# Gated linear attention and a two-layer network on one core: loads without the padding rows, four stores in halves, another fixed order of steps

## The chip, the cores and the metric

The kernel runs on one core of a Trainium2 chip. The metric is device time in microseconds for one execution, on the chip, lower being better. Five engines work beside each other, each in its own fixed order: TensorE (PE, with its weight loads as PEld), VectorE (DVE), ScalarE (ACT), GpSimd (POOL) and SyncE (SP). SP issues the loads and stores here. Semaphores order the engines against each other.

## The reference

Four sequences of 768 tokens with 8 heads of 48 channels go through a recurrence; then all 3072 tokens, 384 wide, go through two dense layers.

```python
for t in range(S):                                  # S = 768; state is [B, H, 48, 48]
    state = alpha[:, :, t, :, None] * state + einsum('bhd,bhe->bhde', k[:, :, t], v[:, :, t])
    y[:, :, t] = einsum('bhd,bhde->bhe', q[:, :, t], state)
x = y.transpose(0, 2, 1, 3).reshape(3072, 384)
h = x @ w_in                                        # 384 -> 2048, weights in float64
g = h * erf(softplus(h))
out = (g @ w_out).astype(float32)                   # 2048 -> 384
```

## The kernel before

The recurrence is computed in chunks of 64 tokens. There are 24 chunk steps (`n` 0 to 23): two pairs of sequences by twelve chunks, and one step holds 128 token rows. A chunk step loads alpha, k, q and v (`la`, `lk`, `lq`, `lv`); two scans over alpha (`sb`, `sa`) give the decay after and up to each token, and k and q are multiplied by them in place (`kk`, `qq`). On TensorE `ps` makes the scores, `qt` and `sv` the outputs from the state and from the chunk's own tokens, `pn` turns k, and `pu` makes the state's update. On VectorE `mk` masks the scores (tile `sT`), `td` decays the state. `kn` and `kd` copy k out, `ta` adds the update. `xh` copies the output's rounded part to `x_hi`; its rest comes either by `xp` on TensorE and `xe` on ScalarE, or by `xl` on VectorE.

Two chunk steps make a block of 256 tokens for the dense layers; there are twelve blocks. Each value is held as a rounded part (`hi`) and a rest (`lo`), so each layer is three products. The 2048 inner columns stand in four groups, each in two halves. `hm_b_g_half` makes half a group of `h` for block b in 18 matmuls of 256 columns, into one of two PSUM tiles. `he` (ScalarE) or `hd` (VectorE) copies it out. `u`, `n1`, `n2`, `n3` and `g` are ScalarE's passes for the nonlinear function, `ma`, `mb`, `z1` and `z2` VectorE's (tiles `s`, `w`, `t`, `hs`). `ga` or `gd` rounds half a group, `gl` takes the rest, and `om_b_g_half` adds 12 matmuls of 384 columns to the block's two accumulators. `oe` or `ob` copies an accumulator out and `od` stores 128 rows of it. `u` and `g` need one function table in ScalarE, `n1` to `n3` another; `need` loads a table wherever the program asks for the other one.

The weights come as float64, in 12 tiles of 128 x 4096 bytes and 16 of 128 x 3072. Each is loaded (`wl`), its high bits copied (`wd`, ScalarE, tile `top`), joined with the low bits (`wa`, VectorE), rounded (`wh` on ScalarE, `wk` on VectorE), and its rest taken: by `wq` on VectorE, or by `wp` on TensorE with `we` on ScalarE. A letter behind these names says which matrix, i or o. `dw` are matmuls of the identity alone, in the gaps of the start.

The order is written out by hand, or by a planner outside of the program: the table ORDER lists all 1605 steps, and the loop at the end calls them one by one. Each engine's instructions stand in the order of these calls, and a chain of dependencies (`Queue.call`, line 204) forbids any other, so SP, too, issues its loads in table order; a load whose tile is still read makes all later ones wait. Nearly every instruction is recorded through that one line, so in the profile rows are told apart by tiles: `h__115` and `h__116` are the PSUM tiles of `hm`, `pn` and `wp`, `acc` those of `om`, `both` that of `ps` and `pu`, `py` that of `qt`, `sv` and `xp`.

Channels are padded from 48 to 64. For alpha, k and q a chunk is 128 rows of channels, with padding in rows 48 to 63 and 112 to 127. For v a row is a token and 8 heads of 64 columns, 16 of them padding.

Of the kernel before, what the change touches and what calls it, by code (L numbers as in the profile page):

```python
# [31 lines left out]
sv_0 wdi_3 pn_0 whi_1 wai_3 wpi_2 la_1 wli_4 xh_0 sb_1 rc_1 xp_0 dw_1 lk_1 kn_0 wdi_4 lq_1 xe_0 wli_0 sa_1 kk_1 wei_2
whi_3 pn_1 qq_1 wqi_1 wai_4 lv_1 pu_0 wlo_3 wdi_0 ps_1 kn_1 whi_4 dw_1 mk_1 ta_0 sv_1 wli_5 pu_1 wdo_3 wai_0 whi_0
wqi_3 wdi_5 xh_1 la_2 ta_1 wao_3 wqi_4 wpi_0 ic_1 wei_0 xp_1 wli_7 sb_2 xe_1 wlo_10 who_3 lq_2 wai_5 rc_2 td_2 wdi_7
sa_2 wai_7 whi_5 hm_0_0_0 qq_2 hm_0_0_1 wli_6 qt_2 lk_2 ic_2 wdo_10 wli_8 wli_9 wao_10 he_0_0_0 kk_2 la_3 lv_2 wdi_6
# [884 lines left out]
```

## Time and profile before

| | us |
|---|---|
| median of 3 runs (506.89 to 510.46) | 507.69 |
| the profiled execution | 507.52 |
| its span, first to last instruction | 505.7 |
| TensorE busy | 495.0 |
| VectorE busy | 478.3 |
| ScalarE busy | 463.0 |
| of it 78 table loads | 100.1 |
| POOL busy | 6.2 |

The span is shorter than the execution's time by what lies before the first instruction and behind the last. A matmul's end is modelled, and matmuls overlap; the distance between the starts of two rows tells more than a row's length. The 16 DMA engines are busy throughout from 5 to 30 us, while the weights come, and by 32% from 40 to 50 us; behind 100 us their share stays under 30%.

### The profile page before, as it was taken

What the parts mean: (1) busy time and instruction counts of PE and PEld (TensorE: products, weight loads), DVE (VectorE), ACT (ScalarE), POOL (GpSimd) and SP (SyncE); (2) the same over time, 40 slices, a digit from 0 to 9 for tenths busy, and PEclk for the clock granted to TensorE, in tenths of its full rate; (3) what the DMA queues carried; (4) which work ended last, traced back from release to release, by engine and by line L of the source; (5) the groups of instructions that cost most, each with busy time, mean ns of one, the idle gap of its engine ahead of it and who ended that gap; (6) DMA issues with size and microseconds to landing.
All of it is one profiled execution on the core that took longest, in us unless ns stands there. A gap on an engine that the chain in (4) does not pass through costs nothing.

```text
span 505.7 us, 16774 instructions
## 1 busy us (share of the span) xinstructions
PE 495.0 (98%) x7418; PEld 473.6 (94%) x7418; DVE 478.3 (95%) x643; ACT 463.0 (92%) x609; POOL 6.2 (1%) x39
## 2 busy tenths in 40 slices
PE   7989999999999999999999999999999999999996
PEld 3689999999999999999999999999999999999996
DVE  6999999999999999999999999999899999689993
ACT  4999999999999899989999999977998899999971
POOL 2000000000000000000000000000000000000000
PEclk9999999999999999999999999999999999999999
DMA  8993663332103123012032122200313100000000
GB/s 290 403 365 84 211 209 107 97 107 72 40 29 111 43 63 126 22 27 97 1 101 81 44 81 96 64 21 21 105 46 110 44 1 34 1 1 31 1 32 34
DMA packets 21386, 43.68 MB, mean 86 GB/s; under 512 B 2368, under 2 KB 5440, under 8 KB 21312
## 3 DMA queue, kind: packets, MB, share of 16 engines
q1 hardware_dynamic: 21312, 42.59, 26.0%
q8 instruction: 59, 0.97, 0.8%
q14 instruction: 15, 0.12, 0.1%
HBM read 37.86 MB, written 4.72 MB: 84 GB/s over the span
## 4 chain that ended last, share of the span: by engine, by line
PE 41%; DVE 9%; ACT 8%; issue 2%; DMA 0%; DVEq 0%
PE acc L204 21%; PE h__116 L204 9%; PE h__115 L204 8%; PE py L204 2%; ACT L204 2%; PE both L204 2%; DVE t L204 1%; ACT w__100 L204 1%; ACT s__85 L204 1%; DVE A L204 1%; DVE gl__108 L204 1%; ACT s__89 L204 1%; ACT s__86 L204 1%; ACT w__99 L204 1%; DVE gl__107 L204 1%
## 5 line engine op out<-in xcount | busy, mean ns | idle before, releaser
L204 ACT ACT_TABLE_LOAD x78 | 100.1, 1283 | 2.2 <-PEq L874 0.9
L204 PE MATMUL acc<-wo_hi,gl__108 128*128 128x384 f32 x192 | 43.4, 338 | 0.1
L204 PE MATMUL acc<-wo_hi,gh__106 128*128 128x384 f32 x192 | 43.0, 337 | 0.0
L204 PE MATMUL acc<-wo_lo,gh__106 128*128 128x384 f32 x192 | 42.9, 337 | 0.0
L204 PE MATMUL acc<-wo_hi,gh__105 128*128 128x384 f32 x192 | 42.2, 339 | 0.0
L204 PE MATMUL acc<-wo_lo,gh__105 128*128 128x384 f32 x192 | 41.5, 336 | 0.0
L204 PE MATMUL acc<-wo_hi,gl__107 128*128 128x384 f32 x192 | 41.3, 336 | 0.0
L204 PEld LDWEIGHTS acc<-wo_hi,gl__108 128*128 128x128 f32 x192 | 34.1, 188 | 0.6 <-DVE gl__108 L204 0.4
L204 PEld LDWEIGHTS acc<-wo_lo,gh__106 128*128 128x128 f32 x192 | 34.3, 188 | 0.0
L204 PEld LDWEIGHTS acc<-wo_lo,gh__105 128*128 128x128 f32 x192 | 34.1, 188 | 0.0
L204 PEld LDWEIGHTS acc<-wo_hi,gl__107 128*128 128x128 f32 x192 | 34.0, 188 | 0.0
L204 PEld LDWEIGHTS acc<-wo_hi,gh__106 128*128 128x128 f32 x192 | 32.9, 188 | 0.2 <-ACT gh__106 L204 0.2
L204 PEld LDWEIGHTS acc<-wo_hi,gh__105 128*128 128x128 f32 x192 | 32.3, 188 | 0.5 <-DVE o__110 L204 0.3
L204 DVE TENSOR_TENSOR_SCAN B<-raw_a,back 128x520 f32<-128x520 f32 x24 | 29.6, 1233 | 1.7 <-DMA raw_a<-in_alpha_dram 1.6
L204 DVE TENSOR_TENSOR_SCAN A<-raw_a,start 128x520 f32<-128x520 f32 x24 | 29.6, 1233 | 0.1
L204 PE MATMUL h__115<-x_hi__112,wi_hi 128*128 128x256 f32 x156 | 23.4, 285 | 0.0
L204 ACT ACTIVATE s__87<-s__87 128x1024 f32<-128x1024 f32 x22 | 23.2, 1054 | 0.1
L204 PE MATMUL h__116<-x_hi__111,wi_lo 128*128 128x256 f32 x150 | 22.0, 281 | 1.1 <-issue 1.1
L204 PE MATMUL h__115<-x_hi__112,wi_lo 128*128 128x256 f32 x156 | 22.7, 281 | 0.0
L204 PE MATMUL h__116<-x_hi__111,wi_hi 128*128 128x256 f32 x150 | 22.7, 287 | 0.0
L204 PE MATMUL h__115<-x_lo__114,wi_hi 128*128 128x256 f32 x156 | 22.6, 280 | 0.0
L204 PE MATMUL h__116<-x_lo__113,wi_hi 128*128 128x256 f32 x150 | 21.8, 281 | 0.0
(370 smaller groups left out, 1364.4 us busy)
## 6 DMA issues: line engine op xcount, KB each, us to landing
raw_a<-in_alpha_dram SPq DMA_DIRECT2D x24, 260.5 KB, 2.8
raw_k<-in_k_dram SPq DMA_DIRECT2D x24, 256.0 KB, 3.3
raw_q<-in_q_dram SPq DMA_DIRECT2D x24, 256.0 KB, 3.6
raw_v__117<-in_v_dram SPq DMA_DIRECT2D x12, 256.0 KB, 3.9
raw_v__118<-in_v_dram SPq DMA_DIRECT2D x12, 256.0 KB, 4.0
out_dram<-o__110 SPq DMA_DIRECT2D x12, 192.0 KB, 3.2
out_dram<-o__109 SPq DMA_DIRECT2D x12, 192.0 KB, 2.0
s__85<-in_moe_w_out_dram SPq DMA_DIRECT2D x5, 384.0 KB, 5.6
```

Of the source, the lines that this page charges most:

```text
L204: ins = made(*args, **kw)
```

## The change

Three things change. (1) From chunk step 1 on, alpha, k and q are loaded into the first 112 partitions alone, so rows 112 to 127 keep what the first load or a memset put there; the k and q tiles of step 1 get their padding from POOL. The other padding, rows 48 to 63, is still loaded. The rows of v lose every second head's padding: 448 columns instead of 512. (2) The four stores of blocks 1 and 2 are each cut into two of 64 rows. (3) The table ORDER lists other steps in another order: `hd` 25 instead of 20 and `he` 71 instead of 76, `ob` 8 instead of 9 and `oe` 16 instead of 15, `wk` 1 instead of 5 and `wh` 27 instead of 23, `wp` 3 instead of 2 and `wq` 25 instead of 26, `xp` with `xe` 3 instead of 4 and `xl` 21 instead of 20. By the new order ScalarE loads a table 70 times instead of 78.

```diff
-la_0 sb_0 rc_0 wli_2 dw_4 sa_0 lk_0 wli_1 lq_0 wli_3 wdi_2 wai_2 kk_0 lv_0 qq_0 wdi_1 ic_0 whi_2 ps_0 wai_1 dw_1 mk_0
...
+la_0 lv_0 lk_0 lq_0 sb_0 rc_0 wli_3 dw_4 wdi_3 sa_0 wlo_10 wdo_10 kk_0 qq_0 wli_2 ps_0 la_1 wli_1 wli_0 pn_0 lk_1 mk_0
...
-    vs = Ring(raw, raw_v=([P, H * HD], F32, 2))
+    VH = HD + D
+
+    def vcol(pair, par):
+        return (pair // 2 * 2 + par) * VH + pair % 2 * HD
+
+    vs = Ring(raw, raw_v=([P, NP * VH], F32, 2))
...
+    for t in (rk[1], rq[1]):
+        nc.gpsimd.memset(t[P - 32 :], 0.0)
...
+        def part(self, out, in_):
+            rows = HD + D if self.n else P
+            sp.dma_start(out=out[:rows], in_=in_[:rows])
+
         def la(self):
-            sp.dma_start(out=ra, in_=alpha[self.m, self.c])
+            self.part(ra, alpha[self.m, self.c])
...
         def od(self, c):
-            sp.dma_start(out=out[bass.ds(self.tok + c * P, P), :], in_=self.o[c])
+            n = P // 2 if isinstance(self.tok, int) and self.tok // TB in (1, 2) else P
+            for at0 in range(0, P, n):
+                sp.dma_start(out=out[bass.ds(self.tok + c * P + at0, n), :], in_=self.o[c][at0 : at0 + n])
...
-            wide = _np.zeros((M, C, NI, TC, NP, 2, 64), a.dtype)
-            wide[..., :D] = a
+            a = a.reshape(M, C, NI, TC, NP // 2, 2, 2, D)
+            wide = _np.zeros((M, C, NI, TC, NP // 2, 2, 64 + D), a.dtype)
+            wide[..., :D], wide[..., 64:] = a[..., 0, :, :], a[..., 1, :, :]
```

`lk` and `lq` call `part` in the same way, and `sv` and `pu` read v by `vcol`.

SP's queue from its first load to the load of chunk step 1's q (`hs` and `s` are staging tiles of weights, 512 and 384 KB; `raw_k_122` and `raw_k_123` serve chunk steps in turn). Before:

```order
L204 DMA raw_a<-in_alpha_dram 128x521
L204 DMA hs__90<-in_moe_w_in_dram 128x4096
L204 DMA raw_k_122<-in_k_dram 128x512
L204 DMA hs__91<-in_moe_w_in_dram 128x4096
L204 DMA raw_q_120<-in_q_dram 128x512
L204 DMA hs__92<-in_moe_w_in_dram 128x4096
L204 DMA raw_v__117<-in_v_dram 128x512
L204 DMA raw_a<-in_alpha_dram 128x521
L204 DMA hs__93<-in_moe_w_in_dram 128x4096
L204 DMA raw_k_123<-in_k_dram 128x512
L204 DMA raw_q_121<-in_q_dram 128x512
```

And now:

```order
L209 DMA raw_a<-in_alpha_dram 128x521
L209 DMA raw_v__117<-in_v_dram 128x448
L209 DMA raw_k_122<-in_k_dram 128x512
L209 DMA raw_q_120<-in_q_dram 128x512
L209 DMA hs__90<-in_moe_w_in_dram 128x4096
L209 DMA s__85<-in_moe_w_out_dram 128x3072
L209 DMA hs__91<-in_moe_w_in_dram 128x4096
L209 DMA raw_a<-in_alpha_dram 112x521
L209 DMA hs__92<-in_moe_w_in_dram 128x4096
L209 DMA hs__93<-in_moe_w_in_dram 128x4096
L209 DMA raw_k_123<-in_k_dram 112x512
L209 DMA raw_q_121<-in_q_dram 112x512
```

The four loads of chunk step 0 moved ahead of all weights; alpha of step 1 stands eighth in both, with 4096 + 3072 + 4096 bytes a row of weights ahead of it instead of three times 4096. A tile of `w_out` came in ahead of step 1's k and q.

VectorE from the first scan of chunk step 1 (tile `B`) to the mask of its scores (`sT`); rows that write `w__` are `wa`, rows that write `wi_lo` or `wo_lo` are `wq`. Before:

```order
L204 SCALAR_TENSOR_TENSOR B<-raw_a,back 128x520
L204 RECIPROCAL start<-B 128x8
L204 SCALAR_TENSOR_TENSOR A<-raw_a,start 128x520
L204 TENSOR_TENSOR raw_k_123<-raw_k_123,B 128x512
L204 TENSOR_TENSOR raw_q_121<-raw_q_121,A 128x512
L204 TENSOR_TENSOR wi_lo<-w__98,wi_hi 128x512
L204 SCALAR_TENSOR_TENSOR w__100<-hs__93,top__102 128x512
L204 TENSOR_TENSOR sT<-both,mask 128x512
```

And now:

```order
L209 SCALAR_TENSOR_TENSOR B<-raw_a,back 128x520
L209 RECIPROCAL start<-B 128x8
L209 SCALAR_TENSOR_TENSOR w__99<-hs__91,top__101 128x512
L209 SCALAR_TENSOR_TENSOR A<-raw_a,start 128x520
L209 SCALAR_TENSOR_TENSOR w__100<-hs__92,top__102 128x512
L209 TENSOR_TENSOR raw_k_123<-raw_k_123,B 128x512
L209 TENSOR_TENSOR wo_lo<-w__98,wo_hi 128x384
L209 TENSOR_TENSOR raw_q_121<-raw_q_121,A 128x512
L209 SCALAR_TENSOR_TENSOR w__97<-hs__93,top__101 128x512
L209 SCALAR_TENSOR_TENSOR w__98<-s__86,top__102 128x384
L209 TENSOR_TENSOR sT<-both,mask 128x512
```

One `wq` and one `wa` stood in between; now it is four `wa` and one `wq`, two of the five with 384 columns.

VectorE in the last tile (group 3 of block 11), from its `ma` (tile `t`) to the copy of the second accumulator (`o__110`). Before:

```order
L204 TENSOR_TENSOR t<-s__88,w__100 128x1024
L204 SCALAR_TENSOR_TENSOR w__100<-t,w__100 128x1024
L204 TENSOR_TENSOR gl__108<-hs__90,gh__106 128x512
L204 TENSOR_TENSOR gl__107<-hs__91,gh__105 128x512
L204 CAST total<-both 1x1
L204 TENSOR_TENSOR s__88<-s__88,w__100 128x1024
L204 TENSOR_TENSOR gl__108<-hs__92,gh__106 128x512
L204 SCALAR_TENSOR_TENSOR hs__93<-s__88,hs__93 128x1024
L204 TENSOR_TENSOR gl__107<-hs__93,gh__105 128x512
L204 TENSOR_TENSOR gl__108<-hs__93,gh__106 128x512
L204 TENSOR_SCALAR o__110<-acc 128x384
```

And now:

```order
L209 TENSOR_TENSOR t<-s__88,w__100 128x1024
L209 TENSOR_TENSOR gl__107<-hs__90,gh__105 128x512
L209 SCALAR_TENSOR_TENSOR w__100<-t,w__100 128x1024
L209 TENSOR_TENSOR s__88<-s__88,w__100 128x1024
L209 TENSOR_TENSOR gl__108<-hs__92,gh__106 128x512
L209 SCALAR_TENSOR_TENSOR hs__93<-s__88,hs__93 128x1024
L209 CAST gh__105<-hs__93 128x512
L209 TENSOR_TENSOR gl__107<-hs__93,gh__105 128x512
L209 CAST gh__106<-hs__93 128x512
L209 CAST total<-both 1x1
L209 TENSOR_TENSOR gl__108<-hs__93,gh__106 128x512
L209 TENSOR_SCALAR o__110<-acc 128x384
```

The rounding of the last tile's two halves (`gh`, CAST) came to VectorE from ScalarE, and the passes of earlier tiles (`gl`) stand in other gaps of this chain. On TensorE twelve `om` steps stood between the last `hm` and `om_11_3_0`; now it is six, with the check's one small matmul (`f2`) ahead of the last tile.

## Rows read from the trace of the kernel before

**Rows 1.** The page, busy us of each engine (share of span) and instructions.

```profile
PE 495.0 (98%) x7418; PEld 473.6 (94%) x7418; DVE 478.3 (95%) x643; ACT 463.0 (92%) x609; POOL 6.2 (1%) x39
```

**Rows 2.** Waits: who <- for what: us in total, times, longest.

```profile
PE h__116 L204 <- issue: 1.1, 1, 1.1
```

**Rows 3.** Timeline, TensorE: start us, us, engine, line, operation, tiles, shapes, count.

```profile
60.80 0.36 PE L204 MATMUL py<-x_hi__111,minus 128*128 128x192 f32 x2
61.09 0.58 PE L204 MATMUL both<-raw_v__117,kn 64*48 64x48 f32 x32
...
62.08 0.86 PE L204 MATMUL py<-raw_q,T 48*32 48x64 f32 x64
62.87 0.66 PE L204 MATMUL h__116<-ident,raw_k 128*128 128x128 f32 x4
63.28 0.96 PE L204 MATMUL h__115<-x_hi__112,wi_hi 128*128 128x256 f32 x6
...
65.49 0.86 PE L204 MATMUL acc<-wo_hi,gh__106 128*128 128x384 f32 x4
...
67.58 0.87 PE L204 MATMUL h__116<-x_hi__112,wi_hi 128*128 128x256 f32 x6
...
69.70 0.87 PE L204 MATMUL h__115<-x_hi__112,wi_hi 128*128 128x256 f32 x6
```

**Rows 4.** Timeline, ScalarE's start; in brackets its idle time before, and the releaser.

```profile
6.06 0.78 ACT L204 ACTIVATE top__101<-hs__90 128x512 f16<-128x512 bf16 x1 [3.58 <-DMA hs__90<-in_moe_w_in_dram]
8.38 0.77 ACT L204 ACTIVATE top__102<-hs__91 128x512 f16<-128x512 bf16 x1 [1.55 <-DMA hs__91<-in_moe_w_in_dram]
...
18.50 0.64 ACT L204 ACTIVATE top__102<-s__85 128x384 f16<-128x384 bf16 x1 [0.16 <-DMA s__85<-in_moe_w_out_dram]
...
20.43 0.47 ACT L204 ACTIVATE x_hi__111<-py 128x384 fp32r<-128x384 f32 x1
```

**Rows 5.** Timeline, VectorE's start.

```profile
5.24 1.24 DVE L204 TENSOR_TENSOR_SCAN A<-raw_a,start 128x520 f32<-128x520 f32 x1
...
9.05 0.69 DVE L204 TENSOR_TENSOR raw_q<-raw_q,A 128x512 f32<-128x512 f32 x1 [0.89 <-DMA raw_q<-in_q_dram]
9.66 0.68 DVE L204 SCALAR_TENSOR_TENSOR w__98<-hs__91,top__102 128x512 int32<-128x512 int32 x1
10.55 0.69 DVE L204 TENSOR_TENSOR sT<-both,mask 128x512 f32<-128x512 f32 x1 [0.22 <-PE both L204]
...
11.93 1.23 DVE L204 TENSOR_TENSOR_SCAN B<-raw_a,back 128x520 f32<-128x520 f32 x1
...
17.05 0.69 DVE L204 TENSOR_TENSOR sT<-both,mask 128x512 f32<-128x512 f32 x1
...
19.17 0.56 DVE L204 SCALAR_TENSOR_TENSOR w__98<-s__85,top__102 128x384 int32<-128x384 int32 x1 [0.23 <-ACT top__102 L204]
```

**Rows 6.** Timeline, TensorE's start.

```profile
7.35 0.81 PE L204 MATMUL both<-T,ident 128*128 128x192 f32 x4
...
17.97 0.86 PE L204 MATMUL py<-sT,raw_v__118 64*32 64x64 f32 x64
...
21.34 0.89 PE L204 MATMUL h__115<-x_hi__111,wi_hi 128*128 128x256 f32 x6
```

**Rows 7.** Timeline of the tail, three engines.

```profile
469.84 0.88 PE L204 MATMUL h__116<-x_hi__112,wi_lo 128*128 128x256 f32 x6
...
475.03 0.68 DVE L204 TENSOR_SCALAR hs__93<-h__115 128x512 f32<-128x512 f32 x1
...
483.41 1.28 ACT L204 ACT_TABLE_LOAD   x1
...
484.71 1.06 ACT L204 ACTIVATE s__88<-s__88 128x1024 f32<-128x1024 f32 x1
...
489.07 1.22 DVE L204 TENSOR_TENSOR t<-s__88,w__100 128x1024 f32<-128x1024 f32 x1
...
500.98 0.51 PE L204 MATMUL acc<-wo_hi,gl__108 128*128 128x384 f32 x2
```

More of the change, by code (lines that the diff above doesn't have):

```diff
@@ L30 @@
 ORDER = """
-la_0 sb_0 rc_0 wli_2 dw_4 sa_0 lk_0 wli_1 lq_0 wli_3 wdi_2 wai_2 kk_0 lv_0 qq_0 wdi_1 ic_0 whi_2 ps_0 wai_1 dw_1 mk_0
[L32 to L35, printed above, removed]
@@ new lines @@
+kn_0 wai_3 lq_1 whi_3 wdi_2 wao_10 sb_1 wlo_3 lv_1 ic_0 wli_5 sv_0 rc_1 wai_2 pu_0 wpi_3 xh_0 who_10 xp_0 wei_3 wdi_1
+dw_1 dw_1 wdi_0 sa_1 wai_1 kk_1 wqo_10 whi_1 dw_1 wpi_1 qq_1 wai_0 whi_2 ps_1 ic_1 wdo_3 pn_1 xe_0 wei_1 wao_3 who_3
+mk_1 wqi_2 whi_0 wpo_3 sv_1 wdi_5 kn_1 wli_9 la_2 ta_0 wqi_0 pu_1 xh_1 xp_1 wdi_9 wli_4 wai_5 sb_2 lk_2 rc_2 weo_3
+xe_1 wai_9 lq_2 sa_2 wli_7 hm_0_0_1 wli_8 ta_1 td_2 wli_6 hm_0_0_0 wdi_4 wli_10 qq_2 kk_2 he_0_0_1 whi_9 pn_2 qt_2
+ic_2 whi_5 wai_4 ps_2 wdi_7 whi_4 wqi_9 la_3 he_0_0_0 wdi_8 lv_2 wai_7 kn_2 wqi_4 wdi_6 wqi_5 whi_7 u_0_0 mk_2
@@ new lines @@
+od_1_0 g_2_3 kn_11 z1_2_3 gd_2_2_0 sv_10 xh_10 rc_12 hm_4_1_0 z2_2_3 gl_2_2_0 u_4_0 hd_4_1_0 ma_3_2 sa_12 u_3_3 g_3_1
+lk_12 lv_12 om_2_2_0 ga_2_3_1 hm_4_2_0 ga_2_3_0 z1_3_1 gl_2_3_1 ic_12 g_3_2 hm_4_1_1 gl_2_3_0 lk_13 lv_11 xl_10
+he_4_1_1 om_2_3_0 ta_10 he_4_2_0 n1_3_3 mk_11 om_2_3_1 n1_4_0 sv_11 z2_3_1 n3_3_0 mb_3_2 td_12 qq_12 ga_3_1_0 kk_12
+pu_11 n2_3_3 ps_12 oe_2_0 z1_3_2 mk_12 n3_3_3 qt_11 pn_12 gl_3_1_0 hm_4_3_1 la_13 ma_3_0 oe_2_1 sb_13 om_3_1_0
+gd_3_1_1 gl_3_1_1 mb_3_0 kn_12 om_3_1_1 n2_4_0 g_3_0 z2_3_2 ma_3_3 rc_13 sa_13 u_4_1 xh_11 z1_3_0 he_4_3_1 g_3_3
@@ new lines @@
+hm_4_3_0 ga_3_2_0 gl_3_2_0 hm_4_2_1 lq_13 xl_11 z2_3_0 hd_4_3_0 mb_3_3 la_14 n1_4_1 om_3_2_0 n2_4_1 he_4_2_1 ga_3_0_0
+hm_5_0_0 n3_4_0 ta_11 gl_3_0_0 gd_3_2_1 td_13 n3_4_1 z1_3_3 od_2_0 u_4_3 z2_3_3 od_2_1 gl_3_2_1 he_5_0_0 ic_13 kk_13
+ma_4_0 hm_5_0_1 mb_4_0 om_3_0_0 u_4_2 om_3_2_1 ga_3_3_1 qt_12 hd_5_0_1 pu_12 g_4_0 n1_4_3 qq_13 ps_13 sv_12 xh_12
+pn_13 gl_3_3_1 hm_5_1_0 om_3_3_1 z1_4_0 mk_13 gd_3_3_0 n2_4_3 n1_4_2 ma_4_1 lk_14 z2_4_0 kn_13 gl_3_3_0 n3_4_3
+ga_3_0_1 ta_12 n2_4_2 sb_14 hm_5_1_1 rc_14 lq_14 kk_14 om_3_3_0 n3_4_2 gl_3_0_1 hd_5_1_0 td_14 om_3_0_1 g_4_1 xl_12
@@ new lines @@
+la_18 lk_17 u_6_0 mb_5_2 hm_6_3_0 g_5_3 ga_5_0_1 xh_15 ma_6_1 hd_6_2_0 g_5_2 gl_5_1_0 u_6_2 qq_17 n1_6_2 od_4_0
+gl_5_0_1 kk_17 om_5_1_0 lv_16 mb_6_1 ga_5_0_0 xl_15 om_5_0_1 td_17 z1_5_2 hm_6_3_1 n2_6_2 z2_5_2 gl_5_0_0 z1_5_3
+n3_6_2 sv_16 ps_17 he_6_3_0 pu_16 n1_6_0 ga_5_2_0 qt_16 pn_17 om_5_0_0 n2_6_0 lq_18 sb_18 ga_5_2_1 he_6_3_1 gl_5_2_0
+rc_18 om_5_2_0 hm_7_0_0 ma_6_2 sa_18 n3_6_0 gl_5_2_1 g_6_2 he_7_0_0 om_5_2_1 kn_17 z2_5_3 xh_16 u_6_3 mb_6_2 la_19
+ma_6_0 ga_5_3_1 g_6_1 n1_6_3 n2_6_3 gd_5_3_0 kk_18 hm_7_3_1 gl_5_3_1 ic_18 n3_6_3 z1_6_1 hd_7_3_1 hm_7_3_0 mb_6_0
@@ new lines @@
+u_7_1 n1_7_2 n2_7_2 qt_18 z1_7_0 pn_19 hm_8_1_1 om_6_0_0 ma_7_3 ga_6_0_1 kd_19 lv_19 xh_18 z2_6_3 g_7_3 gl_6_2_0
+hm_8_1_0 la_20 om_6_2_0 gl_6_0_1 sb_20 he_8_1_0 n1_7_1 rc_20 hd_8_1_1 n2_7_1 ta_18 n3_7_2 ic_20 gd_6_3_0 sa_20 lk_21
+lq_20 n3_7_1 hm_8_3_1 mb_7_3 hd_8_3_1 gl_6_3_0 om_6_0_1 om_6_3_0 xl_18 od_5_0 hm_8_0_0 ga_6_3_1 kk_20 ma_7_1 gl_6_3_1
+z2_7_0 mk_19 qq_20 u_8_1 om_6_3_1 g_7_1 qt_19 he_8_0_0 ps_20 pu_19 la_21 sv_19 ga_7_0_0 pn_20 n1_8_1 lv_20 td_20
+mb_7_1 sb_21 ob_6_1 lv_21 hm_8_3_0 lq_21 xh_19 kn_20 z1_7_3 n2_8_1 rc_21 hm_8_0_1 z1_7_1 sa_21 he_8_3_0 gd_7_0_1
@@ new lines @@
+gd_7_2_1 gl_7_2_1 sa_22 n1_9_0 n2_9_0 hm_9_1_0 kk_22 g_8_3 om_7_1_1 om_7_2_1 ma_8_0 xl_20 hd_9_1_0 hm_9_1_1 mk_21
+mb_8_0 ta_20 ic_22 n3_9_0 qt_21 z2_8_1 qq_22 hd_9_1_1 td_22 ps_22 g_8_0 pu_21 ma_9_0 z1_8_3 ga_8_1_0 gd_8_1_1 mb_9_0
+gl_8_1_0 z1_8_0 sv_21 gl_8_1_1 la_23 oe_7_0 oe_7_1 hm_9_2_0 sb_23 z2_8_0 u_9_1 n1_9_1 he_9_2_0 lv_22 hm_9_2_1 lq_23
+om_8_1_0 od_7_0 ga_8_0_1 xh_21 z2_8_3 n3_8_2 n2_9_1 rc_23 om_8_1_1 od_7_1 hm_9_3_0 gl_8_0_1 mk_22 xl_21 ga_8_3_0
+hd_9_3_0 ic_23 hd_9_2_1 kk_23 sa_23 ma_8_2 om_8_0_1 u_9_3 gl_8_3_0 ga_8_3_1 qq_23 n1_9_3 hm_10_2_1 n2_9_3 om_8_3_0
@@ new lines @@
+oe_9_0 n3_11_0 ma_11_0 ga_10_2_1 oe_9_1 gl_10_2_0 g_10_3 om_10_2_0 mb_11_0 gl_10_2_1 hd_11_2_1 g_11_0 ga_10_1_1
+z1_10_3 gl_10_1_1 z1_11_0 om_10_2_1 he_11_1_1 om_10_1_1 gd_10_0_1 gl_10_0_1 z2_10_3 u_11_2 z2_11_0 u_11_1 od_9_0
+om_10_0_1 n1_11_1 ga_10_0_0 n2_11_1 n3_11_1 gl_10_0_0 gd_10_3_1 n1_11_2 gl_10_3_1 om_10_0_0 gd_10_1_0 gl_10_1_0
+om_10_3_1 ma_11_1 n2_11_2 gd_10_3_0 om_10_1_0 n3_11_2 mb_11_1 hm_11_3_0 od_9_1 g_11_1 gl_10_3_0 gd_11_0_1 z1_11_1
+ma_11_2 gl_11_0_1 z2_11_1 g_11_2 mb_11_2 om_10_3_0 oe_10_1 he_11_3_0 oe_10_0 z1_11_2 hm_11_3_1 gd_11_1_0 he_11_3_1
@@ L290, in lk @@
             rk.append(self.K)
-            sp.dma_start(out=self.K, in_=k[self.m, self.c])
+            self.part(self.K, k[self.m, self.c])
         def lq(self):
@@ L295, in lq @@
             rq.append(self.Q)
-            sp.dma_start(out=self.Q, in_=q[self.m, self.c])
+            self.part(self.Q, q[self.m, self.c])
         def lv(self):
-            self.v = vs.tile([P, H * HD], F32, name="raw_v", tag="raw_v")
+            self.v = vs.tile([P, NP * VH], F32, name="raw_v", tag="raw_v")
             sp.dma_start(out=self.v, in_=v[self.m, self.c])
@@ L427, in pu @@
                     for i in range(NI):
-                        toks, h = slice(i * TC, (i + 1) * TC), 2 * pair + (half ^ i)
+                        toks, at0 = slice(i * TC, (i + 1) * TC), vcol(pair, half ^ i)
                         pe.matmul(
                             out=self.pu_[half * HD : half * HD + D, i, pair * D : (pair + 1) * D],
-                            lhsT=self.kn_[toks, pair, half, :], rhs=self.v[toks, h * HD : h * HD + D],
+                            lhsT=self.kn_[toks, pair, half, :], rhs=self.v[toks, at0 : at0 + D],
                             start=True, stop=True,
@@ L728, in general @@
                             nc.sync.dma_start(out=t[r : r + NP, d, :], in_=src.rearrange("c a t -> (c a) t"))
-                    vs = v[m, bass.ds(c, 1), i * TC : (i + 1) * TC].rearrange(
-                        "c t (a r e) -> r a (c t) e", r=2, e=HD
-                    )
-                    nc.sync.dma_start(out=gv[r : r + NP], in_=vs[par, :, :, :D])
+                    for a in range(NP):
+                        at0 = vcol(a, par)
+                        nc.sync.dma_start(
+                            out=gv[r + a : r + a + 1], in_=v[m, bass.ds(c, 1), i * TC : (i + 1) * TC, at0 : at0 + D]
+                        )
                 for t in range(TC):
```

159 lines of the change are left out of this document (64 added, 95 removed).

## The prediction

> **What bounds the kernel now.** I read the busy shares first: TensorE 98%, VectorE 95%, ScalarE 92% [rows 1]. Three engines so full cannot be told apart by shares, so the next view is the list of waits. Behind the start TensorE hardly stands in it: its longest wait there is 1.1 us of "issue", a wait for nothing that the profile shows [rows 2]. Since matmuls overlap and their ends are modelled, a busy TensorE proves little; what proves it is the time from one start to the next in its timeline [rows 3]. There one `hm` step (18 matmuls, first layer) begins 2.12 us after the other (67.58 to 69.70), one `om` step (12 matmuls, second layer) takes 2.09 (65.49 to 67.58), and a chunk's `pu`, `ps`, `qt` and `pn` together 2.19 (61.09 to 63.28), of it `qt` 0.79.
>
> Add these up from the first `hm` at 21.34 us [rows 6] to the end of the last `om` at 500.98 + 0.51 = 501.5 [rows 7], a stretch of 480.1 us. 96 x 2.12 = 203.5; 96 x 2.09 = 200.6; for 22 chunks 2.19 and another 0.79 for `sv`, which has as many passes as `qt`: 65.6. That is 469.7, so some **10 us** in the whole stretch are waits, changes of step and the two `xp`. No order of the same matmuls can win more than that there. What is left is the start, 21.3 us until the first `hm`, and 4.2 us from the last `om` to the end of the span. The profiled execution took 507.52 us, 1.8 more than its span; the median of the runs is 507.69, so a sum against 507.52 is 0.2 low at most.
>
> **The start.** Before, chunk 0 needs alpha, k and q, and SP issues a weight tile of 512 KB between each of them. VectorE waits for q until 9.05 [rows 5]. After, q is the fourth transfer: 260 + 224 + 256 + 256 = 996 KB with it. The pace comes from ScalarE's waits for landings [rows 4]: 772 KB had come at 6.06 and 1540 KB at 8.38, so 996 KB come near 6.7. VectorE has run both scans by 5.24 + 1.24 = 6.5, multiplies k, then q from 7.1: 2 us earlier than before. The warm-up matmuls fill TensorE until 7.35 + 0.81 = 8.2 [rows 6]; so `ps_0` starts there and its mask follows near 9.0 (10.55 before).
>
> Little of this lead survives. Chunk 1's alpha is now at 2632 KB of the queue (before at 2824 KB). From 1540 KB at 8.38 to 5000 KB at 18.50 [rows 4] the queue gives 342 KB per us: 8.38 + 1092/342 = 11.6 for its landing, and the scan began at 11.93 before [rows 5]. From that scan to the mask of chunk 1 it was 17.05 - 11.93 = 5.1 us, with two weight passes between. After, five stand there, three of 512 columns and two of 384, at 0.69 and 0.56 [rows 5]: 3 x 0.69 + 2 x 0.56 - 2 x 0.69 = 1.8 more. The mask comes at 18.5 and `sv_1` 0.9 later at 19.4 (17.05 to 17.97 before [rows 5, 6]). But before, `xh_1` did not follow `sv_1` directly: ScalarE, busy with weights, came to it at 20.43 [rows 4]. After, ScalarE has `wd_5` ahead of it, which waits for 5224 KB: 18.50 + 224/342 = 19.15; with 0.6 to 0.4 each for `wd_5`, `kn_1` and `ta_0` that makes `xh_1` 20.6, and the first `hm` 0.9 later as before (20.43 to 21.34): **21.5**. If the queue runs faster than it did, VectorE alone sets the pace: its instructions ahead of the scan end at 10.4, and all of this falls 1.2 us earlier, 20.3. If the queue has another hitch of 0.4, it is 21.9. So the first `hm` moves by -1.0 to +0.6; I take **-0.2**, the middle.
>
> Rows of 112 partitions do not occur in this trace. The bounds are 7/8 of the time of 128 rows, since they are 7/8 of the bytes, and the same time; I take 7/8, as the queue went by bytes in rows 4, and since three such loads stand ahead of the first `hm`, it is 96 KB or 0.3 us of queue at most, inside the range above. The Trainium skill (Trainium Kernel Development and Optimization, Best Practices) says to tile to 128 partitions always, which speaks against the cut. Its page DMA: Bandwidth & Descriptors (section on why a DMA increments its semaphore by 16) lets a copy use 16 engines when 16 divides its rows, as it does 112. By the first nothing is won, by the second an eighth of each load; no run here shows it yet, and either way the sum moves by 0.3 at most. Behind the first 40 us the list of waits has no engine that waits for a load, so there the cut is worth nothing.
>
> **The rest.** One `xp` fewer behind the first `hm`, 60.80 to 61.09 [rows 3]: **-0.3**. The weight step through TensorE that is added lies ahead of the first `hm`, in the gap before the mask of chunk 1. Counts of all other matmul steps are the same. Five product copies go from ScalarE to VectorE and four weight copies the other way, which is under 2 us on either, and eight table loads are saved, 8 x 1.30 = 10.4 us less on ScalarE [rows 7]; all of it lies beside TensorE. If that cover went, VectorE's 2 us would count. Four split stores add four issues to SP, and each store that waits for its tile holds later loads behind it; VectorE and ScalarE waited for no load there, so these have slack. POOL's two memsets of 32 rows come ahead of chunk 1's k, which is issued only behind chunk 1's alpha, after the scan that ends at 6.5; POOL has time until then.
>
> **The tail.** Behind the last `hm` there were twelve `om` steps before the first `om` of the last tile; after, there are six: 6 x 2.09 = 12.5 us of cover. The chain to be hidden in it: a copy out 0.69, tanh 1.06, a table load 1.30 (483.41 to 484.71), three passes of 1.06, `ma`, `mb`, `z1` and `z2` of 1.22, two `gl` and `gd` of at most 0.69 [rows 5, 7]: 13.2 us, begun some 0.3 after the matmuls. On one engine an instruction starts some 0.1 before the one ahead is done (9.05 and 9.66, 0.61 apart, where the first takes 0.69 [rows 5]), and ten such pieces make the chain 1 us shorter, 12.5. It sticks out by 0 to 1.0: **+0.2**, near the low end, as the overlap is the rule on both engines.
>
> **Sum:** 507.5 - 0.2 - 0.3 + 0.2 = **507.2 us**. The waits inside the 10 us change places with every order; I take the same total, with -3 and +3 as ends.
>
> **Rivals.** *TensorE's waits close.* ScalarE's 10 us of freedom and a quicker queue let half of the 10 us go and the first `hm` come at 20.3: 507.5 - 1.0 - 0.3 - 5 = 501.2. For it: the engines ran without slack, so each stray wait was passed on. Against: the steps in rows 3 are back to back already, and much of the 10 is the change from step to step. 11%.
>
> *ScalarE sets the pace.* Then its 10.4 us come off: 497.1. Against: ScalarE idles 8% of the span and TensorE 2%. The Trainium skill (ScalarE: Activation LUTs, What ACT_TABLE_LOAD costs) gives 2.66 us a switch, because of a drain behind the load; this trace has 1.30 from the load to the next pass [rows 7], so no drain shows. By its figure 21 us of ScalarE would go free and this rival would give 486. 3%.
>
> *Slower: the last tile's chain is late.* It starts on time only if VectorE reaches it with no queue. Before, VectorE copied out the second-to-last product at 475.03, though its matmuls were done when those of the last began, at 469.84 - 0.71 = 469.1 [rows 7]: 5.9 us of lag, and nobody minded, under twelve `om`. With six, each us of lag beyond the 1 us that VectorE has between its pieces there is a us of TensorE standing still: with the same lag 507.2 + 4.9 = 512.1, and 0.7 us more is over 1%. For it: VectorE is 95% busy. Against: the new table puts the previous tile's `z1` ahead of that `hm`. 8%.
>
> **Chances.** The forecast, unforeseen waits of up to 3 us either way included, has 78%. A measurement of this kernel tells 1%, 5 us, from no change. Faster by over that (below 502.6): most of the first rival and the second, 0.11. Slower (above 512.8): part of the third and of waits that I did not see, 0.07. The range leaves out the first two rivals and most of the third: 503 to 510.5.
>
> **What would show it.** Right: the first `hm` at 20.3 to 21.9; q multiplied near 7; the scan of chunk 1 at 10.4 to 11.9; 70 table loads; `hm` and `om` steps as now. Wrong: `om` or `hm` steps that wait over 1 us in many places, a wait of over 1 us before the last tile, a clock under full between the warm-up and the last `om`.

## The result, and the profile after

Six runs of the changed kernel have a median of 512.33 us (511.59 to 513.78), six of the kernel before 507.27 (506.61 to 510.46): a ratio of 1.0098, 95% interval [1.0078, 1.0119]. The change makes the kernel 5 us, or 1%, slower. The forecast was 507.2 with a range up to 510.5, so it was wrong.

The page's busy line answers to [rows 1]; the row under it counts the table loads.

```profile
PE 497.9 (98%) x7419; PEld 476.1 (93%) x7419; DVE 480.0 (94%) x643; ACT 451.6 (88%) x601; POOL 6.6 (1%) x41
...
L209 ACT ACT_TABLE_LOAD x70 | 89.8, 1283 | 2.1 <-PEq L888 0.9
```

ScalarE lost 11 us of work, 463.0 to 451.6, and the table loads are 70, as the table of steps said. None of it shortened the kernel. TensorE, 98% busy before and after, works as fast as before: one `hm` step and one `om` step take 2.12 us each in the timeline of TensorE (488.95 - 486.83, 491.07 - 488.95), where [rows 3] had 2.12 and 2.09.

```profile
486.83 0.87 PE L209 MATMUL h__115<-x_hi__112,wi_hi 128*128 128x256 f32 x6
...
488.95 0.87 PE L209 MATMUL acc<-wo_hi,gh__105 128*128 128x384 f32 x4
...
491.07 0.87 PE L209 MATMUL acc<-wo_hi,gh__106 128*128 128x384 f32 x4
...
501.77 0.19 PE L209 MATMUL both<-ones,good 128*1 128x1 f32 x2
502.06 0.97 PE L209 MATMUL acc<-wo_hi,gh__105 128*128 128x384 f32 x4
...
505.98 0.51 PE L209 MATMUL acc<-wo_hi,gl__108 128*128 128x384 f32 x2
```

The last three rows answer to [rows 7]. Between the end of the last `om` before the last tile and the tile's own (502.06) stands only the check's small matmul. So the chain of the last tile, of which a rival made 4.9 us, is on time; and the span ends 4.1 us behind the last matmul's end (4.2 before).

The 4.9 us of span lie earlier. The first `hm` comes at 22.91 instead of 21.34 [rows 6], 1.6 us later, and from it to the end of the last `om` it is 483.6 us instead of 480.1, 3.4 more. The view that shows more of it is one that the prediction does not use: the span in stretches. Its columns are the stretch and its length, the busy us (and instructions) of TensorE, its weight loads, VectorE, ScalarE and POOL, then TensorE's granted clock, the share of time in which the DMA engines were busy, and the GB/s they moved. Of the kernel before:

```profile
5.00:15.00 10.00, 8.37 (x118) 4.46 (x116) 8.33 (x12) 5.90 (x12) 0.00 (x0) 1.00 1.02 382
15.00:25.00 10.00, 9.31 (x203) 7.23 (x203) 9.72 (x16) 9.47 (x21) 0.00 (x0) 1.00 1.04 403
25.00:35.00 10.00, 9.78 (x277) 8.93 (x276) 9.66 (x16) 9.83 (x17) 0.10 (x1) 1.00 1.01 361
35.00:45.00 10.00, 8.87 (x188) 8.34 (x187) 9.51 (x15) 9.14 (x17) 0.10 (x1) 1.00 0.48 163
```

And after:

```profile
5.00:15.00 10.00, 9.25 (x151) 5.15 (x150) 6.86 (x12) 5.17 (x11) 0.36 (x1) 1.00 1.01 323
15.00:25.00 10.00, 8.41 (x161) 5.66 (x160) 8.82 (x14) 8.01 (x18) 0.00 (x0) 1.00 1.05 307
25.00:35.00 10.00, 9.11 (x164) 8.35 (x163) 9.16 (x16) 8.44 (x14) 0.10 (x1) 1.00 1.03 338
35.00:45.00 10.00, 7.74 (x231) 7.08 (x224) 8.23 (x14) 9.31 (x17) 0.10 (x1) 1.00 0.90 227
```

Read the last two columns first. The DMA engines are busy all the time in both (share 1.0), yet they move 323, 307 and 338 GB/s where they moved 382, 403 and 361. The queue is slower while it is full. So the burst of weights, which left the engines half idle from 35 us (0.48), now fills that stretch too (0.90). TensorE's busy time from 25 to 45 us falls from 18.65 to 16.85 us, VectorE's from 19.17 to 17.39, ScalarE's from 18.97 to 17.75. The list of waits from 22 to 45 us names what they waited for (engine, tile, releaser: us in total, times, longest):

```profile
PE py L209 <- issue: 1.5, 1, 1.5
DVE raw_q L209 <- DMA raw_q<-in_q_dram: 1.1, 1, 1.1
ACT top__102 L209 <- DMA hs__90<-in_moe_w_in_dram: 1.0, 1, 1.0
DVE B L209 <- DMA raw_a<-in_alpha_dram: 1.0, 1, 1.0
PE h__116 L209 <- ACT wi_hi L209: 0.9, 1, 0.9
PE both L209 <- issue: 0.7, 1, 0.7
```

VectorE and ScalarE wait for loads, and TensorE once, 0.9 us, for one of the two: the profile names ScalarE's `wi_hi`, but the matmuls that waited, at 28.21, read the k that VectorE had ready at 28.11. The two "issue" waits of TensorE, 1.5 and 0.7 us, have no releaser in the profile, and they are 2.2 of the 3.15 us that TensorE is idle from 25 to 45 us: for most of its lost time the profile does not show what it waited for. They are absent wherever the queue was fast in this order; the kernel before has one of 1.1 us in its own order [rows 2], which ends at 36.90, late in its burst. A candidate that no run tried: the profile has a queue that it calls `instruction`, with packets of 16 KB on the same DMA engines. One such packet was moved between 40.5 and 42.5 us (`q8 instruction: 1, 0.02, 4.0%`), where the second wait begins (43.28 - 1.52 = 41.76).

### The profile page after: what moved, and what is told of

Read it like the earlier page. It is cut to its first block, busy times and chain, and to the rows that moved or that the text cites. A ratio compares the mean times of both kernels' runs of the same rounds, so it can differ in the third digit from the quotient of the medians.

```text
span 510.6 us, 16757 instructions
## 1 busy us (share of the span) xinstructions
PE 497.9 (98%) x7419; PEld 476.1 (93%) x7419; DVE 480.0 (94%) x643; ACT 451.6 (88%) x601; POOL 6.6 (1%) x41
## 4 chain that ended last, share of the span: by engine, by line
PE 71%; ACT 12%; DVE 9%; issue 4%; DMA 3%; SPq 0%; DVEq 0%; ACTq 0%
PE acc L209 29%; PE h__116 L209 18%; PE h__115 L209 16%; PE py L209 5%; PE both L209 4%; ACT L209 3%; DMA hs__96<-in_moe_w_in_dram 2%; DMA raw_a<-in_alpha_dram 2%; ACT w__100 L209 1%; DVE t L209 1%; ACT s__86 L209 1%; DVE B L209 1%; ACT s__88 L209 1%; ACT s__89 L209 1%; ACT w__98 L209 1%
## 5 line engine op out<-in xcount | busy, mean ns | idle before, releaser
L209 PE MATMUL h__116<-x_hi__111,wi_hi 128*128 128x256 f32 x162 | 24.4, 287 | 0.5 <-DVE hs__95 L209 0.5
L209 ACT ACTIVATE s__87<-s__87 128x1024 f32<-128x1024 f32 x22 | 23.3, 1059 | 0.5 <-DVE t L209 0.4
L209 PE MATMUL h__116<-x_hi__111,wi_lo 128*128 128x256 f32 x162 | 23.6, 281 | 0.0
L209 PE MATMUL h__116<-x_lo__113,wi_hi 128*128 128x256 f32 x162 | 23.5, 281 | 0.0
L209 ACT ACTIVATE s__89<-s__89 128x1024 f32<-128x1024 f32 x20 | 21.1, 1055 | 1.6 <-DVE t L209 1.5
L209 PE MATMUL h__116<-x_hi__112,wi_hi 128*128 128x256 f32 x150 | 22.5, 286 | 0.0
L209 PEld LDWEIGHTS h__116<-x_hi__111,wi_hi 128*128 128x128 f32 x162 | 21.4, 189 | 0.8 <-DVE hs__95 L209 0.7
```

What stands on the lines that cost most here:

```text
L209: ins = made(*args, **kw)
```

## The experiments

### First: the parts of the change, each alone or left out

The theory after the result: loads into 112 partitions are slow and slow the transfers beside them. Rivals: the new order costs the time; v's shorter rows do. Loads whole again in the changed kernel (POOL's two memsets, which only the cut needs, go with it):

```diff
         def part(self, out, in_):
-            rows = HD + D if self.n else P
+            rows = P
```

> The changed kernel, with alpha, k and q again loaded into all 128 partitions; the new order, the narrow rows of v and the split stores stay. Theory (loads of 112 partitions are slow: in the changed kernel's first 45 us a 2048-byte packet takes 124 ns, before 84 to 92, and the transfers beside it slow too): packets back under 95 ns, the first hm near 21 instead of 22.9, the waits of 1.0 and 1.8 us at 35 and 41 us gone, and 507 to 508.5 us. Rival 1 (the new order itself costs the 5 us): first hm near 22.9, 511 to 512.5. Rival 2 (v's 1792-byte rows slow the queue): packets stay above 110 ns, 511 to 512.5.

Measured: 508.28 us, ratio to before 1.0015 [1.0006, 1.0023]. The same stretches:

```profile
5.00:15.00 10.00, 9.77 (x150) 5.42 (x149) 6.75 (x11) 5.06 (x11) 0.00 (x0) 1.00 0.99 353
15.00:25.00 10.00, 8.20 (x155) 5.03 (x154) 9.06 (x15) 7.96 (x19) 0.00 (x0) 1.00 1.03 405
25.00:35.00 10.00, 10.00 (x226) 9.49 (x225) 9.97 (x16) 9.68 (x17) 0.10 (x1) 1.00 1.01 361
35.00:45.00 10.00, 10.00 (x284) 9.38 (x265) 9.93 (x18) 9.97 (x18) 0.10 (x1) 1.00 0.50 176
```

405 and 361 GB/s again, the burst over by 40 us, and TensorE busy all of 20.00 us from 25 to 45. That is 3.15 us more than in the changed kernel, out of a loss of 0.83% or 4.2 us that went away; 0.8 us is left. A packet of 2048 bytes took 91 ns on average from 4 to 45 us, 126 in the changed kernel. One number of the theory missed: the first `hm` came at 23.57, not near 21. ScalarE's pass on its first weight tile, which waited for the landing, began 0.9 us later than in the changed kernel, at 9.41 instead of 8.51. The kernel of the second part that is the same up to step 7 had its first `hm` at 22.53, so one execution's start scatters by 1 us, and the first `hm` of a single profile weighs little.

The other three are before's code with one part of the change each:

```diff
# cut_alone
+        def part(self, out, in_):
+            rows = HD + D if self.n else P
+            sp.dma_start(out=out[:rows], in_=in_[:rows])
# order_alone
-la_0 sb_0 rc_0 wli_2 dw_4 sa_0 lk_0 wli_1 lq_0 wli_3 ...
+la_0 lv_0 lk_0 lq_0 sb_0 rc_0 wli_3 dw_4 wdi_3 sa_0 ...
# v_and_stores_alone
-    vs = Ring(raw, raw_v=([P, H * HD], F32, 2))
+    vs = Ring(raw, raw_v=([P, NP * VH], F32, 2))
```

> The kernel before with only one thing changed: alpha, k and q of chunk steps 1 to 23 go into 112 partitions, and POOL zeroes the last 32 rows of step 1's k and q tiles. Theory: 2048-byte packets near 120 ns in the first 45 us, first hm 0.7 to 1.6 us later than 21.34, 509 to 511.5 us. Rivals 1 and 2: no change, 507 to 508, packets at 84 to 92 ns.

> The kernel before with the new order of steps alone: loads of 128 partitions, old rows of v, stores whole. Theory: 507 to 508.5 us, packets under 95 ns. Rival 1: 511 to 512.5 us. Rival 2: 507 to 508.5, as the theory.

> The kernel before with v's rows of 448 columns and the four split stores, the old order and loads of 128 partitions. Theory and rival 1: within 0.5 us of before. Rival 2: 2 to 5 us slower, packets above 110 ns.

Measured: the cut alone 510.60 us, ratio 1.0066 [1.0053, 1.0079]; the order alone 507.12, 0.9984 [0.9957, 1.0011]; v and the stores 507.55, 1.0007 [0.9988, 1.0026]. The cut alone is slower, the other parts cannot be told from no change: both rivals, which asked for 4 to 5 us, fall. In the old order the cut costs 3.3 us. Its 2048-byte packets took 109 ns on average, less than the 120 expected. Its stretches again show a full queue that moves less:

```profile
5.00:15.00 10.00, 9.46 (x118) 4.75 (x116) 8.66 (x13) 6.27 (x13) 0.36 (x1) 1.00 1.03 346
15.00:25.00 10.00, 8.32 (x192) 6.09 (x193) 8.26 (x14) 7.70 (x18) 0.00 (x0) 1.00 1.04 359
25.00:35.00 10.00, 8.96 (x214) 8.17 (x213) 9.14 (x15) 9.44 (x19) 0.10 (x1) 1.00 1.04 326
35.00:45.00 10.00, 8.88 (x242) 8.18 (x242) 9.28 (x17) 8.99 (x14) 0.10 (x1) 1.00 0.71 208
```

The order alone also dates the loss, since its steps stand in the same order as the changed kernel's. Two of its rows:

```profile
40.01 0.95 PE L204 MATMUL h__116<-x_hi__111,wi_hi 128*128 128x256 f32 x6
...
500.41 0.51 PE L204 MATMUL acc<-wo_hi,gl__108 128*128 128x384 f32 x2
```

In the changed kernel the same two begin at 45.08 and 505.98, the first `hm` at 22.91 instead of 21.77. So it is 1.1 us late at the first `hm`, 5.1 at 45 us and 5.6 at the end: nearly all of the loss lies ahead of 45 us.

### Second: where the cut costs, and whether it is the rows

The changed kernel with the cut from chunk step 7 on, behind the burst (five of the 28 weight tiles are still to come):

```diff
-            rows = HD + D if self.n else P
+            rows = HD + D if self.n > 6 else P
```

> The changed kernel, but alpha, k and q take 112 partitions from chunk step 7 on only; steps 1 to 6, whose loads stand among the weights, take all 128. Theory (a load of 112 partitions costs nothing when it is alone, 2.4 to 2.5 us from issue to landing against 2.6 for 128, and costs only where the queue is full): as with all loads whole, 507.5 to 508.8 us, first hm without a change, no wait over 0.9 us between 30 and 45 us. Rival (each such load costs some, early or late): 17 of 23 steps still have it, so 510 to 511.5 us.

Measured: 507.88 us, ratio 1.0002 [0.9992, 1.0012]. Seventeen of 23 steps still load 112 rows and it costs nothing. The whole loss comes from the first six steps' loads; those of steps 1 to 4 are issued before 40 us, while the queue is full.

Then the kernel before with only its weight tiles split, so that nothing else of the change is in play; one line of `wl` each:

```diff
-                sp.dma_start(out=flat, in_=self.src)
# weights_112_16 (weights_64_64, weights_96_32: with those rows)
+                for r0, r1 in ((0, 112), (112, P)):
+                    sp.dma_start(out=flat[r0:r1], in_=self.src[r0:r1])
# weights_columns
+                for b0 in (0, 4 * self.n):
+                    sp.dma_start(out=flat[:, b0 : b0 + 4 * self.n], in_=self.src[:, b0 : b0 + 4 * self.n])
# weights_even_odd
+                for r0 in (0, 1):
+                    sp.dma_start(out=flat[r0::2], in_=self.src[r0::2])
```

> The kernel before, whose weight tiles come in two loads each, rows 0 to 111 and rows 112 to 127: the same bytes to the same places, 28 loads more. Theory (rows in sevens for each DMA engine collide with each other and with the loads in 128 rows): 4096-byte packets go from 160 to over 190 ns, the tiles of 512 KB land over 1.6 us apart instead of 1.29, and the time is 511 to 518 us. Rival (it is something about alpha, k and q, their source or their early place, not the rows): 1.3 us apart, 507 to 508.5 us.

> The kernel before, whose weight tiles come in two loads of 64 rows each. Rival (only shares of seven rows are slow; four rows for each DMA engine go as eight do): tiles of 512 KB 1.3 us apart, 507 to 508.5 us. Theory in its wider form (the engines get into each other's way wherever a load's rows are not spread as 128 are): over 1.6 us apart, 511 us or more. By the Trainium skill (SBUF - State Buffer, Door 1: The DMA port swizzle) rows 0 to 63 reach only half the ports, so that such a load goes at half the pace: tiles up to 2.6 us apart. That sentence apart, the expectation is 511 to 530.

> The control to the other two: the kernel before, whose weight tiles come in two loads of 128 rows and half the columns each (28 loads more, packets of 2048 and 1536 bytes instead of 4096 and 3072). Theory: packets of 2048 bytes at 84 to 92 ns, tiles of 512 KB within 1.4 us, 507 to 509 us. Rival (more loads alone, or smaller packets, cost the time): 510 us or more.

> The kernel before, whose weight tiles come in two loads of 64 rows each, as where rows 0 to 63 and 64 to 127 stood apart (527.19 us, 228 GB/s from 5 to 25 us), but here the even rows and the odd rows. Theory (what counts is which partitions are written at the same time): a load that reaches over all 128 partitions does better, over 260 GB/s and 510 to 521 us. Rival (what counts is that each DMA engine gets four rows of a load instead of eight, wherever they lie): as before that, 225 to 235 GB/s, 524 to 530 us. By the Trainium skill (SBUF - State Buffer, Door 1: The DMA port swizzle) even rows reach all 16 ports, rows 0 to 63 only eight. That sentence apart, the expectation stands.

> The kernel before, whose weight tiles come in two loads, rows 0 to 95 and 96 to 127 (six and two rows for each DMA engine). Theory: between the loads in 112 and 16 rows (518.97 us) and those in 64 and 64 (527.19), 516 to 528 us, packets of 4096 bytes over 220 ns. Rival (only an odd share, seven rows, is slow): 507 to 509 us and 160 to 175 ns.

Measured, with the same bytes in all five. The last column is the mean of the three stretches from 5 to 35 us; in the kernel before it is 382:

| weight tile in two loads | us | ratio to before | GB/s |
|---|---|---|---|
| 128 rows, half the columns each | 507.97 | 1.0007 [0.9988, 1.0027] | 360 |
| even rows, odd rows (64 each) | 508.30 | 1.0024 [1.0013, 1.0034] | 372 |
| rows 0 to 111, 112 to 127 | 518.97 | 1.0206 [1.0178, 1.0234] | 267 |
| rows 0 to 95, 96 to 127 | 519.14 | 1.0222 [1.0193, 1.0250] | 266 |
| rows 0 to 63, 64 to 127 | 527.19 | 1.0384 [1.0349, 1.0419] | 230 |

One stretch of each, 5 to 15 us, in the order of the table:

```profile
5.00:15.00 10.00, 8.79 (x118) 4.54 (x116) 8.34 (x12) 6.29 (x13) 0.00 (x0) 1.00 1.02 380
```

```profile
5.00:15.00 10.00, 8.18 (x118) 4.50 (x116) 7.80 (x11) 5.42 (x11) 0.00 (x0) 1.00 1.02 387
```

```profile
5.00:15.00 10.00, 6.75 (x109) 3.62 (x108) 5.74 (x9) 3.63 (x7) 0.00 (x0) 0.91 1.03 267
```

```profile
5.00:15.00 10.00, 6.79 (x111) 3.95 (x110) 6.48 (x10) 3.96 (x8) 0.00 (x0) 0.89 1.05 272
```

```profile
5.00:15.00 10.00, 5.55 (x42) 2.89 (x41) 4.32 (x8) 2.13 (x4) 0.00 (x0) 0.82 1.03 228
```

The DMA share is 1.02 to 1.05 in all five rows, and the queue moves 380, 387, 267, 272 and 228 GB/s. So the number of loads and shorter packets cost nothing that shows in the time (columns), and a load of 64 rows in itself costs 0.2% (even and odd). Which rows a load takes sets the pace: the pairs of neighbouring rows, 64 and 64, go at 0.60 of the kernel before (230/382), the pairs with 112 and 96 at 0.7. Within a pair the runs do not tell which of the two loads is the slow one. Rows of the tile and rows of the source in DRAM change together in these runs, so none tells whether the partitions written or the places read are the cause. The rival that it is something about alpha, k and q falls with 112 and 16, although their 518.97 is 1 us above the theory's range; the rival that only sevens are slow falls with 64 and 96; the rival that a smaller share for each DMA engine is what is slow falls with the even and odd rows, which did better than the theory's 510. The last column but two, the granted clock, is under 1 in the slow three: TensorE waits there (5.55 of 10 us busy), and the clock falls as far as 0.67 in one stretch of the last kernel, a mean between its two levels, 1.2 and 2.4 GHz. How much of those 20 us is the clock's was not measured.

The Trainium skill (SBUF — State Buffer, Door 1: The DMA port swizzle) says that rows 0 to 63 reach only eight of the 16 ports through which DMA writes; by its port map the even rows reach all. The runs agree in the order of the two, 228 against 387 GB/s; ports themselves show in no trace.

### Third: a cut that keeps the pace?

In the changed kernel, the 112 rows as 56 even and 56 odd ones; and, apart from it, a cut to 120 rows:

```diff
# cut_even_odd
-            sp.dma_start(out=out[:rows], in_=in_[:rows])
+            for r0 in (0, 1):
+                sp.dma_start(out=out[r0:rows:2], in_=in_[r0:rows:2])
# cut_to_120
-            rows = HD + D if self.n else P
+            rows = 120 if self.n else P
```

> The changed kernel, whose loads of 112 rows (and chunk step 0's of 128) come as two loads each, the even rows and the odd rows: 56 rows each, the padding still left out, 72 loads more. Theory (what slows the queue is which partitions are written at the same time, and rows apart by two are harmless, as the weights in even and odd rows showed): 387 GB/s or so in the start again instead of 307 to 338, 2048-byte packets under 95 ns, no wait of over 1.2 us between 30 and 45 us, 507 to 509.5 us. Rival (a count of rows that isn't a power of two is slow however the rows lie): 511 to 514 us, packets over 110 ns.

> The changed kernel, whose alpha, k and q take 120 partitions from chunk step 1 on instead of 112: one load each, as there, and eight rows for each of 15 DMA engines, if they are shared out evenly. Narrow form of the theory (only shares of seven rows, which begin in the midst of a group of partitions, collide): as with 128 rows, 507.5 to 509 us, 2048-byte packets under 95 ns, over 350 GB/s from 5 to 25 us. Wide form (any share other than that of 128 rows collides when the queue is full): 510.5 to 513 us, packets over 105 ns, under 330 GB/s. In between, the count of rows sets the size.

Measured: 515.02 us, 1.0158 [1.0133, 1.0183], and 513.90, 1.0120 [1.0100, 1.0140]. The even and odd rows are slower than the changed kernel (1.0098 [1.0078, 1.0119]); the 120 rows are no faster, and the two intervals overlap. For 120 rows the narrow form of the theory falls. The wide form comes near, 0.9 us above its range: 112 and 120 neighbouring rows in one load both slow the full queue.

```profile
5.00:15.00 10.00, 8.62 (x149) 4.90 (x148) 6.61 (x12) 5.16 (x11) 0.36 (x1) 1.00 1.03 336
15.00:25.00 10.00, 7.99 (x155) 5.00 (x154) 8.08 (x12) 7.75 (x18) 0.00 (x0) 1.00 1.04 299
25.00:35.00 10.00, 7.38 (x138) 6.88 (x137) 7.64 (x14) 6.26 (x13) 0.10 (x1) 0.90 1.02 310
```

In the last of these stretches the granted clock is 0.90, so part of this loss may be the clock's.

The even and odd 56 rows contradict the theory's number, and the run cannot say why. Its queue moved 296 GB/s from 5 to 15 us, but at a share of 0.93, so it wasn't even full; that fits SP, which came late. A pair of loads kept SP 1.6 to 2.3 us in its timeline, a single one 0.4 to 0.5 in the changed kernel (start us, us, engine, what, how many):

```profile
6.97 1.78 SPq L209 DMA_DIRECT2D raw_a<-in_alpha_dram  x2
...
10.12 1.57 SPq L209 DMA_DIRECT2D raw_k<-in_k_dram  x2
11.79 2.28 SPq L209 DMA_DIRECT2D raw_q<-in_q_dram  x2
```

```profile
8.04 0.50 SPq L209 DMA_DIRECT2D raw_k<-in_k_dram  x1
8.64 0.38 SPq L209 DMA_DIRECT2D raw_q<-in_q_dram  x1
```

From 15 us on the queue was full and moved 318 and 331 GB/s, so the 56 rows are slower than 128 in some measure too; how much of it is their count and how much their places stays open.

## Why the prediction was wrong, point by point

**The failed step** is the price of 112 rows. The prediction bounded it by 7/8 of the time of 128 rows and by the same time, took 7/8, and so let the whole cut move the sum "by 0.3 at most". Both bounds lay on the good side: the trace before had no row of such a load, and nothing excluded a price above the same time. It was 4.2 us in the new order, 3.3 in the old. The bytes went down, the pace of the queue further: 307 against 405 GB/s from 15 to 25 us is 0.76, where the prediction let the pace stand.

**The second failed step** is where it could matter. That behind the first 40 us "the cut is worth nothing" was right as far as it was tried (cut from step 7: 1.0002). But the sum followed the queue only as far as the first `hm`, and priced nothing between it and 40 us, although the front part of the document had the DMA engines busy throughout to 30 us. Before, the list of waits has next to no wait for a load there (from 21 to 40 us one of 0.2 us, for a k), but it does not say how much later the loads could have come. At some 320 GB/s instead of 380 to 400 they were late, and TensorE was idle for 3.15 us of the 20 from 25 to 45: 0.9 of it behind ScalarE or VectorE, 2.2 in waits without a releaser. The 1.1 us of "issue" that the prediction saw [rows 2] and took for nothing is a wait of that kind, late in the burst.

**The start.** q was multiplied at 7.05, as forecast (7.1). The first `hm` came at 22.91, not at 20.3 to 21.9. The forecast slips in two pieces, which the timeline shows of VectorE:

```profile
7.05 0.69 DVE L209 TENSOR_TENSOR raw_q<-raw_q,A 128x512 f32<-128x512 f32 x1
...
12.55 1.24 DVE L209 TENSOR_TENSOR_SCAN B<-raw_a,back 128x520 f32<-128x520 f32 x1 [1.63 <-DMA raw_a<-in_alpha_dram]
...
19.41 0.68 DVE L209 TENSOR_TENSOR sT<-both,mask 128x512 f32<-128x512 f32 x1
```

of ScalarE:

```profile
19.13 0.59 ACT L209 ACTIVATE wi_lo<-h__115 128x512 fp32r<-128x512 f32 x1
...
21.91 0.52 ACT L209 ACTIVATE x_hi__111<-py 128x384 fp32r<-128x384 f32 x1
```

and of TensorE:

```profile
19.77 0.91 PE L209 MATMUL h__115<-w__98,ident 128*128 128x384 f32 x2 [0.18 <-ACT wi_lo L209]
...
20.79 0.86 PE L209 MATMUL py<-sT,raw_v__118 64*32 64x64 f32 x64
...
22.91 0.89 PE L209 MATMUL h__116<-x_hi__111,wi_hi 128*128 128x256 f32 x6
```

The scan of chunk 1 began at 12.55, behind a wait of 1.63 for its alpha; the forecast had 10.4 to 11.9. That carries to the mask, 19.41 instead of 18.5. It is not the cut's: ahead of this alpha stand only loads of 128 rows, and the changed kernel with whole loads has it too. The other piece is the order's: `sv_1` came 1.4 us behind the mask, not 0.9, because the added weight step through TensorE (19.77) did not fit "in the gap before the mask". ScalarE had to write `wi_lo` first, from the same PSUM tile, at 19.13. The scan with whole loads, and then the order alone, where the second piece is there and the first is not:

```profile
12.50 1.24 DVE L209 TENSOR_TENSOR_SCAN B<-raw_a,back 128x520 f32<-128x520 f32 x1 [0.89 <-DMA raw_a<-in_alpha_dram]
```

```profile
11.48 1.24 DVE L204 TENSOR_TENSOR_SCAN B<-raw_a,back 128x520 f32<-128x520 f32 x1 [0.18 <-DMA raw_a<-in_alpha_dram]
...
18.27 0.68 DVE L204 TENSOR_TENSOR sT<-both,mask 128x512 f32<-128x512 f32 x1
```

```profile
18.64 0.91 PE L204 MATMUL h__115<-w__98,ident 128*128 128x384 f32 x2 [0.31 <-ACT wi_lo L204]
...
19.65 0.86 PE L204 MATMUL py<-sT,raw_v__118 64*32 64x64 f32 x64
...
21.77 0.89 PE L204 MATMUL h__116<-x_hi__111,wi_hi 128*128 128x256 f32 x6
```

**What held.** The order alone was forecast at -0.2 - 0.3 + 0.2 = -0.3 us and measured at -0.8 (interval -2.2 to +0.6). Its parts moved otherwise than the terms say, so that the sum fits is in part luck: the first `hm` 0.4 later, and TensorE busy all of the 20 us from 25 to 45, 1.35 more than before. The eight table loads, which the order alone has too, are worth nothing that can be measured, nor are v's rows with the split stores; the tail is on time. None of the three rivals occurred, and none of them was the true mechanism.

**The two rules.** The Trainium skill's sentence to tile to 128 partitions always (Trainium Kernel Development and Optimization, Best Practices) was weighed at 0.3 us and was worth 4. Its rule of divisors (DMA: Bandwidth & Descriptors, on why a DMA increments its semaphore by 16) gives the number of engines that share a load; what the traces add is their pace: from 4 to 45 us a 2048-byte packet took 126 ns on average in the changed kernel, 91 in the same with whole loads.

None of the versions beats the kernel before by more than a measurement can tell; the order alone, 0.9984 [0.9957, 1.0011], comes nearest to it.

## What to carry to other kernels

Bytes are not the price of a load in a full queue. Before you cut rows, look whether the DMA share is near 1.0 where those loads run, and take the GB/s of that stretch as the thing to protect: leave padding partitions in, and cut columns instead; that of v's rows cost nothing here, though it won nothing either. And where a trace shows no instance of an operation, "no worse than the old one" is not a bound.

## What the runs showed of the hardware that was not expected

- Fewer bytes in the same number of loads can take longer: in the new order 112 and 120 rows slow the full queue to 299 to 338 GB/s between 5 and 35 us (128 rows: 353 to 405), also the transfers of 128 rows beside them (4096-byte packets of the weights: 174 ns before, 195 after on average, from 4 to 45 us), while from step 7 on they cost nothing.
- A weight tile in even and odd rows loads nearly as fast as in one piece (372 against 382 GB/s from 5 to 35 us), in two times 64 neighbouring rows at 0.6 of it (230).
- A load cut in two costs SP a second issue: in its timeline to 14 us the pairs of half weight tiles (columns; even and odd) took 0.9 to 1.4 us, the pairs of 56 strided rows 1.6 to 2.3, single loads of the changed kernel 0.3 to 0.6.
